# Seven block products for eight in half of a two-layer attention kernel

## The chip, the cores and the metric

The kernel runs on one core of a Trainium2 chip. The metric is the device time of one launch in microseconds (us). TensorE multiplies, VectorE and ScalarE do the elementwise work, GpSimd masks and issues loads, SyncE (SP) and ScalarE issue other transfers. Inputs and outputs are float32.

## The reference

Two attention layers over their own input, each with 2048 rows, 1024 columns, 32 heads of 32, side by side in the output:

```python
qkv = x @ wqkv                     # 2048x1024 @ 1024x3072
# layer A: each row attends to itself and 7 earlier rows, 2 apart
idx = pos[:, None] - arange(8)[None, :] * 2
logits = einsum("bhsd,bhswd->bhsw", q, k[idx]) * 32 ** -0.5     # idx < 0 masked
# layer B: each row attends to itself and the 255 rows before it
scores = einsum("bhqd,bhkd->bhqk", q, k) * 32 ** -0.5           # other keys masked
out = (softmax(...) applied to v) @ wo                          # @ 1024x1024
return concatenate([a, b], axis=-1)
```

## The kernel before, in words

**Units.** Rows are cut into units of 512. Units 0 to 3 are layer B (dense: a head needs 256 keys for a row), units 4 to 7 are layer A. Layer A's rows are put in another order on the host, even rows first, so that "2 apart" becomes "neighbours": units 4 and 5 are the even rows, 6 and 7 the odd ones. Features are worked on in eight groups of 128, which are four heads each; in this text one such group of one unit is a "head".

**Projections.** A float32 value is split in a high part (a cast to fp32r) and a low part (the difference), and each product is three matmuls: high-high, high-low, low-high (`TERMS`). For a unit, each of the 8 feature groups takes a product for q and one for k (L518, 8 pieces of 128 of the contraction times three terms, 512 columns: 24 matmuls), the values v come in three parts (L583, with 512 or 256 columns), and 8 output products (`o_items`, L645, 24 matmuls each) multiply the attention's results by `wo`. `qk_items`, `v_items` and `o_items` write these. A product fills one PSUM bank; there are three banks for products (`7 - NS`), four for scores, one for a head's values.

**The stream.** Weights and x come from DRAM through one stream (class `Stream`) with three buffers `raw` of 128x1024 (512 KB, `NRAW`). `load_to` issues a load on GpSimd's queue (L159), `split_to` casts what has landed (L201 on ScalarE or L204 on VectorE) and subtracts for the low part (L207 on VectorE). A buffer is loaded again once it has been split.

**Attention.** A head of layer A (`window`): scores (L711, 128 matmuls of 32x40), a mask added (L719), softmax on four passes over 128x640 on VectorE and an exponential on ScalarE (L735 to L747), a transpose (L749), eight copies on ScalarE that spread the weights (L758, L761), 40 matmuls with v (L774). Two sets of buffers alternate. The result is copied (L822, high part on ScalarE) and its low part made (L826, VectorE), and stays in SBUF for the output products. q, k and v of layer A stay on the chip too.

**The order.** The kernel is written out by a planner while it is built. It keeps a clock for each engine from fixed costs, holds four sequences (projections `gemm`, first and second halves of heads, others), and always puts next on TensorE what can start first by its clocks. What follows a product (eviction, low parts, sums) is written when the clocks say it is due. On the chip each engine then runs its instructions in that fixed order and waits on semaphores where data is late.

```python
def copy_out(dst, ps, bank, ring):
    if max(ck.free["act"], ck.now) + 0.48 <= max(ck.free["dve"], ck.now) + 0.6:
        nc.scalar.copy(dst, ps)
```

`copy_out` is an example: whether ScalarE or VectorE empties a bank is settled by the planner's clocks.

Of the kernel before, what the change touches and what calls it, by code (L numbers as in the profile page):

```python
# [25 lines left out]
LIGHT, LIGHT_FROM = 0.5, (4, 1)  # L26
# [8 lines left out]
TAIL, XAT = 4, 1  # L35
# [95 lines left out]
class Stream:  # L131
# [3 lines left out]
    def __init__(self, nc, ck, raws, wpool, xpool, items, more, light):  # L135

        self.nc, self.ck, self.raws, self.wpool, self.xpool, self.more = nc, ck, raws, wpool, xpool, more
        self.items = items
        self.raw, self.tiles, self.ready = {}, {}, {}
        self.loaded = self.split = 0  # L140
        self.light = light
        self.load_to(NRAW + len(more))

    def load_to(self, n):
        while not self.loaded:
# [7 lines left out]
            self.loaded = 2  # L153
        while self.loaded < min(n, len(self.items)):
            k = self.loaded - NRAW
# [3 lines left out]
            (self.nc.scalar if early else self.nc.gpsimd).dma_start(raw if len(ap.shape) == 2 else raw.rearrange("p (a b) -> p a b", a=2), ap)  # L159
            self.raw[self.loaded] = raw, (self.ck.load if early else self.ck.fetch)("load", self.ck.now)  # L160
            self.loaded += 1

    def split_to(self, n):
        while not self.split:
            (rx, tx), (rw, tw) = self.raw.pop(0), self.raw.pop(1)
            self.tiles[0], self.ready[0], self.ready[1] = [], [], []
            w = self.tiles[1] = self.wpool.tile([P, 2, 1024], F32R, tag="w", name="w")
            for h in range(2):
                c = slice(h * S, h * S + S)
                self.tiles[0].append(self.xpool.tile([P, 2, S], F32R, tag="x", name="x"))  # L170
# [5 lines left out]
        while self.split < min(n, len(self.items)):  # L176
            i = self.split
            self.load_to(i + 1)
            raw, t0 = self.raw.pop(i)
            if self.items[i][0] != "w":  # L180
                self.tiles[i], self.ready[i] = [], []
                for h in range(2):
                    t = self.xpool.tile([P, 2, S], F32R, tag="x", name="x")
                    self.ready[i].append(self.parts(t, raw[:, h * S:(h + 1) * S], t0, i < SIDE))
                    self.tiles[i].append(t)
            else:
                t = self.wpool.tile([P, 2, 1024], F32R, tag="w", name="w")
# [3 lines left out]
            end = self.ready[i] if self.items[i][0] == "w" else max(self.ready[i])  # L191
# [18 lines left out]

    def get(self, i):
# [5 lines left out]
def kernel(ctx, tc, xs, wqk, wv, wo, outs, units):  # L217
# [3 lines left out]
    U = len(units)  # L221
    units, xs = [units[i] for i in ORDER], [xs[i] for i in ORDER]
# [3 lines left out]
    wpool = ctx.enter_context(tc.tile_pool(name="wpool", bufs=3))  # L226
    xpool = ctx.enter_context(tc.tile_pool(name="xpool", bufs=NX))
    natp = ctx.enter_context(tc.tile_pool(name="natp", bufs=NN))
    pickp = ctx.enter_context(tc.tile_pool(name="pickp", bufs=1))
    opool = ctx.enter_context(tc.tile_pool(name="opool", bufs=NO))  # L230
# [13 lines left out]
    for u in range(U):  # L244
        for s in range(NG):
            if u and s in O_SLOTS:
                plan += [("o", u - 1, n) for n in O_SLOTS[s]]
# [4 lines left out]
        if u + 1 < U:  # L252
            plan.append(("x", u + 1))
    plan += [("o", U - 1, n) for n in range(NG)]
    items, where = [], {}

# [13 lines left out]
    for p in plan:  # L270
        ly = units[p[1]][0]
        if p[0] == "o":
            item(p, "w" if p[1] < U - 1 or p[2] < 3 else "xw", wo[ly, p[2]])
# [8 lines left out]
        elif p[0] == "qk":  # L282
            for t in range(2):
                if p + (t,) not in where:
                    item(p + (t,), "w", wqk[ly, 2 * p[2] + t])
        else:
            if NG - 1 in V_SLOTS:
                item(("qk", p[1], 0, 0), "w", wqk[units[p[1]][0], 0])
                unit_x(p[1])
            else:  # L290
                unit_x(p[1], 0)
                item(("qk", p[1], 0, 0), "w", wqk[units[p[1]][0], 0])
                unit_x(p[1], 1, 2, 3)
# [3 lines left out]
    st = Stream(nc, ck, raws, wpool, xpool, items, [more[:, 1024 * i:1024 * i + 1024] for i in range(3)],  # L297
                where[("qk",) + LIGHT_FROM + (0,)] if LIGHT_FROM[0] < U else len(items))

# [831 lines left out]
```

## Time and profile before

| | |
|---|---|
| median of 3 runs | 1833.96 us (1833.75 to 1835.53) |
| span of the profiled execution | 1830.6 us |
| that execution's own time | not given; the median is 3.4 above the span |
| TensorE busy | 1807.8 us, 99% |
| VectorE, ScalarE, GpSimd busy | 1202.9, 889.4, 394.4 us |
| DMA | 257.43 MB, mean 141 GB/s |
| layer A's part | from about 1030 us to the end |

The page first gives each engine's busy time and its share of the span; then the span in forty slices; then the DMA queues; then the chain of work that ended last, followed back from the end, by engine and line; then the groups of instructions, with busy time, mean and the idle time ahead of them. "L518" is line 518 of the kernel. Other views (busy time by window, the timeline, groups with shapes kept apart) are answers of the same trace.

### The profile page before, as it was taken

What the parts mean: (1) busy time and instruction counts of PE and PEld (TensorE: products, weight loads), DVE (VectorE), ACT (ScalarE), POOL (GpSimd) and SP (SyncE); (2) the same over time, 40 slices, a digit from 0 to 9 for tenths busy, and PEclk for the clock granted to TensorE, in tenths of its full rate; (3) what the DMA queues carried; (4) which work ended last, traced back from release to release, by engine and by line L of the source; (5) the groups of instructions that cost most, each with busy time, mean ns of one, the idle gap of its engine ahead of it and who ended that gap; (6) DMA issues with size and microseconds to landing.
All of it is one profiled execution on the core that took longest, in us unless ns stands there. A gap on an engine that the chain in (4) does not pass through costs nothing.

```text
span 1830.6 us, 38331 instructions
## 1 busy us (share of the span) xinstructions
PE 1807.8 (99%) x14826; PEld 1477.5 (81%) x14826; DVE 1202.9 (66%) x2694; ACT 889.4 (49%) x2254; POOL 394.4 (22%) x926
## 2 busy tenths in 40 slices
PE   9999999999999999999999999999999999999998
PEld 7787777888778888788887788888888788888887
DVE  6677886768867669777777564655547445655463
ACT  5556466565655655656555343433425234423331
POOL 3322323233242324332233200110001000100000
PEclk9999999999999999999999999999999999999999
DMA  8455665545656456455554343444334443534432
GB/s 242 121 138 139 176 164 150 170 121 160 164 155 164 136 151 183 125 157 141 141 142 130 110 135 116 152 143 130 119 115 143 133 138 108 162 107 128 127 104 83
DMA packets 109141, 257.43 MB, mean 141 GB/s; under 512 B 14496, under 2 KB 29856, under 8 KB 108960
## 3 DMA queue, kind: packets, MB, share of 16 engines
q0 software_dynamic: 41760, 152.06, 28.1%
q1 hardware_dynamic: 56832, 83.00, 17.6%
q10 hardware_dynamic: 10368, 19.93, 3.0%
q8 instruction: 117, 1.92, 0.5%
q14 instruction: 64, 0.52, 0.1%
HBM read 164.63 MB, written 23.07 MB: 103 GB/s over the span
## 4 chain that ended last, share of the span: by engine, by line
PE 92%; DVE 4%; DMA 2%; ACT 2%; issue 1%; SPq 0%; ACTq 0%; POOL 0%; DVEq 0%; POOLq 0%
PE g L518 37%; PE g L645 19%; PE g L583 17%; PE s L940 5%; PE s L857 5%; PE o L987 5%; PE s L711 2%; PE o L774 2%; DMA raw<-xs 1%; DVE w L207 1%; DVE s L862 1%; ACT s L867 0%; DMA qst<-nat 0%; DMA pbuf<-nat 0%; DVE x L207 0%
## 5 line engine op out<-in xcount | busy, mean ns | idle before, releaser
L518 PE MATMUL g<-x,w 128*128 128x512 f32 x3072 | 770.2, 394 | 3.8 <-DVE nm L729 2.4
L518 PEld LDWEIGHTS g<-x,w 128*128 128x128 f32 x3072 | 566.3, 189 | 114.2 <-issue 8.3
L583 PE MATMUL g<-w,x 128*128 128x256 f32 (+1 forms) x2304 | 391.9, 320 | 0.9 <-issue 0.7
L207 DVE TENSOR_TENSOR w<-raw,w 128x512 fp32r<-128x512 f32 x516 | 338.6, 698 | 52.0 <-ACT w L201 44.8
L583 PEld LDWEIGHTS g<-w,x 128*128 128x128 f32 x2304 | 332.3, 190 | 29.2 <-DVE w L207 1.8
L645 PE MATMUL g<-ot,w 128*128 128x512 f32 x1416 | 343.6, 393 | 3.7 <-DVE ot L826 1.8
L867 ACT ACTIVATE s<-s,nm 128x384 f32<-128x384 f32 (+2 forms) x512 | 274.3, 536 | 102.1 <-DVE nm L862 101.8
L862 DVE CUSTOM_DVE_ANT_0 s<-s,mask_d 128x384 f32<-128x384 f32 (+2 forms) x512 | 261.5, 553 | 88.2 <-PE s L857 87.5
L645 PEld LDWEIGHTS g<-ot,w 128*128 128x128 f32 x1416 | 262.4, 188 | 59.3 <-DVE ot L826 3.2
L926 POOL TENSOR_SCALAR_AFFINE_SELECT pbuf<-pbuf 128x128 f32<-128x128 f32 (+1 forms) x606 | 219.8, 391 | 325.1 <-ACT pbuf L947 323.8
L947 ACT ACTIVATE pbuf<-s 128x384 f32<-128x384 f32 (+2 forms) x480 | 202.7, 505 | 72.2 <-PE s L940 70.2
L159 POOL DMA_DIRECT2D raw<-wqk x126 | 68.1, 540 | 457.5 <-DVE w L207 356.3
L204 DVE CAST w<-raw 128x1024 fp32r<-128x1024 f32 x205 | 141.7, 691 | 24.8 <-PE g L518 24.0
L940 PEld LDWEIGHTS s<-qst,kst 128*128 128x128 f32 x704 | 113.0, 188 | 41.2 <-ACT s L867 16.3
L857 PE MATMUL s<-kst,qst 96*128 96x384 f32 (+2 forms) x512 | 142.4, 342 | 0.9 <-ACT s L867 0.6
L940 PE MATMUL s<-qst,kst 128*128 128x256 f32 (+2 forms) x704 | 136.5, 302 | 3.5 <-ACT s L867 3.0
L719 DVE TENSOR_TENSOR band<-s,near 128x160 f32<-128x160 f32 x128 | 32.4, 315 | 158.0 <-PE s L711 158.0
L536 ACT COPY ost<-g 128x512 f32<-128x512 f32 x54 | 31.7, 587 | 207.1 <-PE g L645 200.4
L857 PEld LDWEIGHTS s<-kst,qst 96*128 96x128 f32 x512 | 93.4, 189 | 26.2 <-issue 4.7
L826 DVE TENSOR_TENSOR ot<-o,ot 128x512 fp32r<-128x512 f32 x64 | 44.0, 688 | 101.6 <-ACT ot L822 101.4
L867 ACT ACTIVATION_READ_ACCUMULATOR s<-s,nm 128x1 f32 x512 | 105.3, 206 | 0.0
L159 POOL DMA_DIRECT2D raw<-wo x64 | 34.2, 534 | 304.2 <-DVE w L207 260.2
(77 smaller groups left out, 1298.6 us busy)
## 6 DMA issues: line engine op xcount, KB each, us to landing
raw<-wqk POOLq DMA_DIRECT2D x126, 512.0 KB, 4.3
raw<-wv POOLq DMA_DIRECT2D x72, 512.0 KB, 5.1
raw<-wo POOLq DMA_DIRECT2D x64, 512.0 KB, 4.1
qst<-nat SPq DMA_DIRECT2D x96, 256.0 KB, 5.3
kst<-nat SPq DMA_DIRECT2D x96, 256.0 KB, 5.6
raw<-xs POOLq DMA_DIRECT2D x28, 512.0 KB, 4.6
outs<-ost ACTq DMA_DIRECT2D x56, 256.0 KB, 2.3
kst<-halo SPq DMA_DIRECT2D x72, 128.0 KB, 4.5
```

The costliest lines, as they stand in the source:

```text
L159: (self.nc.scalar if early else self.nc.gpsimd).dma_start(raw if len(ap.shape) == 2 else raw.rearrange("p (a b) -> p a b", a=2), ap)
L204: nc.vector.tensor_copy(t[:, 0, :], raw)
L207: nc.vector.tensor_tensor(t[:, 1, c:c + 512], raw[:, c:c + 512], t[:, 0, c:c + 512].bitcast(F32), op=ALU.subtract)
L518: nc.tensor.matmul(h["ps"], h["w"][:, a, k * P:(k + 1) * P], xt[u][k][:, b, :], start=(k == 0 and i == 0), stop=(k == NK - 1 and i == 2))
L583: nc.tensor.matmul(ps, xt[u][kw * g + k][:, a, p0:p0 + P], h["w"][g][:, c, k], start=(first and t == 0 and half == 0), stop=(last and t == 2),
L645: nc.tensor.matmul(h["ps"], w[:, a, c:c + P], ot[u, k][:, b, :], start=(k == 0 and i == 0), stop=(k == NK - 1 and i == 2))
L857: nc.tensor.matmul(ps[:, :n], q[0:96, j, b * P:(b + 1) * P], kk[0:96, j, c0:c1], start=True, stop=True)
L862: nc.vector.tensor_tensor_reduce(ps[:, :n], ps[:, :n], mask[:, cut:full], scale=-1.0, scalar=BIG, op0=ALU.add, op1=ALU.min, accum_out=nm)
L867: nc.scalar.activation(ps[:, :n], ps[:, :n], AF.Exp, bias=nm, scale=-1.0, accum_out=sm)
L926: nc.gpsimd.affine_select(w, w, pattern=[[0, m], [step, n]], compare_op=ALU.is_ge, fill=0.0, base=base, channel_multiplier=chan)
L940: nc.tensor.matmul(ps[:, i * n:(i + 1) * n], kk[:, j, 256 + kb * P:256 + (kb + 1) * P], q[:, j, q0:q0 + n], start=True, stop=True)
L947: nc.scalar.activation(w, ps[:, :pack * n].rearrange("p (j n) -> p j n", j=pack), AF.Exp)
```

## The change

Layer A's products are made in Strassen's manner. The rows of two units (1024 rows: units 4 and 5 are the first pair, 6 and 7 the second) and the 1024 x 1024 matrices of q with k, of v and of `wo` are cut into 2 x 2 blocks. In place of eight block products there are seven (Winograd's form): four sums of blocks on each side, seven products, and seven sums of the results.

```python
PRODUCTS = (("11", "11"), ("12", "21"), (0, 3), (2, 2), ("22", 1), (3, 0), (1, "22"))
PAIRS = {"x": ((0, 1), (2, 3), (5, 6), (4,)), "o": ((0, 1), (4,), (2, 3), (5, 6))}
GROUPS = (("q", (0, 1, 2)), ("v", (0, 1, 2, 3)), ("q", (3, 4, 5)), ("q", (6, 7)))
FIRST = (("q", (0, 1, 2)), ("q", (3, 4, 5)), ("q", (6, 7)), ("d", (0, ..., 7)), ("v", (0, 1, 2, 3)))
PACE = ((70, 5.0), (154, 2.0))
SUMS = (("21", "+22", "-11"), ("12", "-S0"), ("11", "-21"), ("21", "+22"))
```

- **Groups.** A product of blocks is worked off in groups: 4 pieces of the contraction x 3 terms = 12 matmuls of 512 columns into one PSUM bank. "q" has 8 groups a product (q and k together), "v" and "o" (outputs) 4. `PAIRS` sets the order of products (numbers 0 to 6, "p0" to "p6"), two at a time; `GROUPS` the order within such a two. A pair's q, k and v are 84 groups, its outputs 28. The order is: q, k, v of the first pair (groups 0 to 91, the 8 output products "d" of layer B's last unit among them); of the second pair (92 to 175); outputs of the first (176 to 203), of the second pair (204 to 231). `FIRST` is the order at the first two products of the first pair: all q and k, then "d", then v.
- **Sums of weights** are made by VectorE during layer B (`spare_sums`, 24 tasks of two loads, four sums and a store) and for `wo` in two background lanes from the last dense head on, and kept in DRAM (`td`).
- **Sums of x and of attention results** (`SUMS`, four per pair and side) are made when they are needed: the blocks come through the stream's three `raw` buffers and `combine` adds or subtracts them in place (L256). Sum 0 is stored to DRAM too (`keep_sum`) and loaded again for sum 1 ("-S0").
- **Evictions.** `evac` copies a group out of its bank (L999) or adds it to an accumulator in SBUF (L1005); where two products are added to one another they stay in one bank.
- **Through DRAM.** q, k and v go to DRAM (`qkd`, `vd`) and are fetched for each head (`fetch`), not earlier than `PACE` allows: a head of the first pair every 5 groups from group 70, of the second pair every 2 groups from group 154. Attention results go to DRAM (`od`), are loaded again through the stream and split there (in layer B, L822 and L826's way stays).
- **Due times.** Each entry of the stream has a group number from which on it is split or summed; `phase_done` is called at the end of each group, behind `evac`; for the eight output products "d" it is called ahead of `copy_out`.

```diff
+    def combine(self, raw, t0, sign):
+        part, t1 = self.part
+        self.nc.vector.tensor_tensor(raw, part, raw, op=ALU.add if sign == "+" else ALU.subtract)
+        return raw, self.ck.use("dve", 1.25, t0, t1, port=True)
...
+            if self.items[i][0] == "p":
+                self.part = raw, t0
...
+            if self.items[i][0] in "+-":
+                raw, t0 = self.combine(raw, t0, self.items[i][0])
...
+            out += [(max(free, use[k][0] - S_AHEAD), use[k][0], 1, k + (z,)) for z in range(2)]
...
+    def keep_sum(raw, t, kind, u, z):
+        nc.sync.dma_start(sums[kind, u][:, 2 * z:2 * z + 2, :], raw.rearrange("p (a b) -> p a b", a=2))
...
+                if u == DU - 1:
+                    phase_done(phases.index(("d", u, n)))
                 o = stp.tile([P, S], F32, tag="ost", name="ost")
                 e = copy_out(o, h["ps"], h["b"], rg)
...
+            for t, (a, c) in enumerate(TERMS):
+                if b == "v":
+                    l, r = x[:, a, P * n:P * n + P], w[:, c, :]
+                else:
+                    l, r = w[:, a, P * k:P * k + P], x[:, c, :]
+                nc.tensor.matmul(h["ps"], l, r, start=(half == 0 and k == 0 and t == 0), stop=(k == 3 and t == 2),
+                                 skip_group_check=True)
+
+        def after(k):
+            if k < 3:
+                return
+            evac(kind, u, p, b, n, h)
+            phase_done(f)
...
+        if p == 0:
+            e = move(a)
+        elif p == 1:
+            o, key = out_tile()
+            e = move(o)
+            put(0, 0, o, e, key)
+        elif p == 2:
+            e = add(acc_u(b, n), a)
+        elif p == 3:
+            e = add(a, a)
...
+    def phase_done(f):
+        bg["at"] = f + 1
+        st.split_to(upto[f])
+        fetch()
...
+            if max(hg - 2, last_dense) not in done["scores"] or any((m,) + x not in done["c"] for x in need) or \
+                    bg["at"] < first + step * (r * NG + s):
+                break
...
-    n = TAIL
-    tail = [gemm[len(gemm) - NG * NK + i * NK:len(gemm) - NG * NK + (i + 1) * NK] for i in range(NG)]
...
+    for f, ph in enumerate(phases):
+        gemm += o_items(ph[1], ph[2]) if ph[0] == "d" else phase_items(f)
```

In `combine`, `part` is the block that came first. The work in layer B (units 0 to 3) keeps its order, with the weights' sums between.

More of the change, by code (lines that the diff above doesn't have):

```diff
@@ new lines, with landed @@
+    qkd = {(u, g): dram.tile([P, 2, 2 * S], F32, name=f"qk{u}_{g}") for u in range(DU, U, 2) for g in range(NG)}
+    vd = {(u, j): dram.tile([P, 8, S], F32, name=f"vd{u}_{j}") for u in range(DU, U, 2) for j in range(2)}
+    done = {}
+    for k in ("stack", "v", "o", "ot", "out", "nat", "second", "clear", "scores", "s", "t", "c"):
+        done[k] = {}
+    gates = {}
+    def landed(key, *which):
+        return lambda: all(done[key].get(w, ck.now + 1) <= ck.now for w in which)
+    phases = []
@@ L354 @@
     halo = [[dram.tile([P, 2, 256], F32, name=f"halo{i}_{s}") for s in range(NG)] for i in range(2)]
[L356 to L359 removed]
+    xt, xready, ot, rows, waiting = {}, {}, {}, {}, {}
     class Ring:
```

588 lines of the change are left out of this document (479 added, 109 removed).

## The prediction

> **What bounds the kernel now.** I read the page first, then the busy time by stretch, then the groups by form, then single stretches of the timeline.
>
> ```profile
> span 1830.6 us, 38331 instructions
> PE 1807.8 (99%) x14826; PEld 1477.5 (81%) x14826; DVE 1202.9 (66%) x2694; ACT 889.4 (49%) x2254; POOL 394.4 (22%) x926
> ...
> PE 92%; DVE 4%; DMA 2%; ACT 2%; issue 1%; SPq 0%; ACTq 0%; POOL 0%; DVEq 0%; POOLq 0%
> ```
>
> TensorE is busy for 1807.8 of 1830.6 us and holds 92% of the chain that ended last. Only 22.8 us are idle, so nothing but fewer or cheaper matmuls can shorten this kernel, and every new pause of TensorE is paid in full. The busy time of layer A alone, from 1030 us to the end (each row: the window, then busy time and instructions of PE, PEld, DVE, ACT and POOL, the granted clock, the share of the DMA engines, GB/s):
>
> ```profile
> 1442.00:1640.00 198.00, 195.61 (x2141) 162.37 (x2140) 109.50 (x188) 73.21 (x138) 20.55 (x37) 1.00 0.43 130
> ...
> sum 801.00, PE 789.44 PEld 656.57 DVE 440.45 ACT 293.20 POOL 77.20; mean PE 197.36 PEld 164.14 DVE 110.11 ACT 73.30 POOL 19.30
> ```
>
> There TensorE has 789 of 801 us, VectorE 440 (55%), the DMA engines a share of 0.43 in the row shown. The other engines have room; the question is whether the new work can use it without holding up TensorE.
>
> **What is removed.** The groups of TensorE between 1442 and 1640 us, and one row of the chain:
>
> ```profile
> L518 PE MATMUL g<-x,w 128*128 128x512 f32 x373 | 87.8, 392 | 0.0
> ...
> L583 PE MATMUL g<-w,x 128*128 128x256 f32 x192 | 23.9, 284 | 0.0
> ...
> 1688.17 10.88 PE g L518 x48
> ```
>
> Forty-eight matmuls of 512 columns take 10.88 us in a row, 0.2267 each; one of 256 columns costs 23.9/192 = 0.1245. In the listing of the built program the 512-column products of x, weights and attention outputs number 5376 before and after, and the 256-column ones fall from 1536 to 768: layer A had 2688 of the wide and 768 of the narrow, and has 2688 wide, exactly seven eighths. So the change does what it says, and TensorE loses 768 x 0.1245 = 95.6 us. The attention's own matmuls are unchanged in number. If nothing else happened, the span would be 1735.0.
>
> **What is added, and why it lies on the path.** A group now has 12 matmuls, 2.7 us. There are three PSUM banks for groups, so TensorE can run about two groups, 5.4 us, past an eviction that doesn't come. Evictions, and the sums of x or of attention outputs (`combine`, 1024 columns on VectorE), stand in one order on VectorE and ScalarE. `phase_done` issues all sums that are due by then in one go, each behind its load, and there are only three buffers for loads. This is ScalarE's and VectorE's order at the first such place, with the loads on GpSimd, from the listing (not a profile):
>
> ```
> ACT  902 L243 TensorCopy x<-raw 128x512 [waits DMASW4_49,DVE_49]
> ACT  904 L243 TensorCopy x<-raw 128x512 [waits DMASW7_49,DVE_49]
> ACT  906 L718 TensorCopy ost<-g 128x512 [waits DMAHW2_49]
> DVE  1927 L256 TensorTensor raw<-raw 128x1024 [waits DMASW4_49,DVE_49]
> DVE  1930 L256 TensorTensor raw<-raw 128x1024 [waits DMAHW5_49,DMASW7_49,DVE_49]
> POOL 737 L182 DMACopy raw<-xs 128x1024 [waits DMASW3_49,DVE_49]
> POOL 738 L182 DMACopy raw<-xs 128x1024 [waits DMAHW5_49,DMASW4_49,DVE_49]
> ```
>
> The eviction at 906 had its data long before, but stands behind four casts, the last two of which wait for a sum (1930), that waits for a load (738), that waits for the store of the previous sum out of the same buffer (DMAHW5). That a ready instruction sits behind a waiting one is seen in the trace of before too:
>
> ```profile
> 1716.78 0.59 ACT L822 CAST ot<-o 128x512 fp32r<-128x512 f32 x1 [5.08 <-PE o L774]
> ...
> 1718.34 1.29 DVE L207 TENSOR_TENSOR w<-raw,w 128x512 fp32r<-128x512 f32 x2 [3.29 <-ACT w L201]
> 1719.55 0.68 DVE L826 TENSOR_TENSOR ot<-o,ot 128x512 fp32r<-128x512 f32 x1
> ```
>
> L826's input was there at 1717.37; it ran at 1719.55, behind L207 that waited 3.29 us for another cast. The prices of the steps:
>
> ```profile
> DMA to landing us min/median/max: 3.6/4.5/9.3
> ...
> outs<-ost ACTq DMA_DIRECT2D x56, 256.0 KB, 2.3
> ...
> L747 DVE TENSOR_TENSOR band<-band,sm 128x640 f32<-128x640 f32 x32 | 26.4, 825 | 1.1
> ...
> L826 DVE TENSOR_TENSOR ot<-o,ot 128x512 fp32r<-128x512 f32 x64 | 44.0, 688 | 101.6 <-ACT ot L822 101.4
> ...
> L201 ACT CAST x<-raw 128x512 fp32r<-128x512 f32 x31 | 17.8, 618 | 22.7 <-DMA raw<-xs 19.9 <-DVE x L204 2.6
> ```
>
> A load of the stream (512 KB) lands 4.5 us after its issue; ends 3.6 and, under load, 6. A sum of 1024 columns: 0.825 x 1024/640 = 1.3 (no such operation was in the trace; between 0.7, one cast of that width, and 1.4, two of L826; the row of the same kind decides). Two casts 1.2, their low parts run beside or behind. A store of 512 KB is bounded by one of 256 KB (2.3) and a load (4.5); I take the middle, 3.4. An eviction with an add is L826's 0.69, a copy 0.6.
>
> The first place, from the end of the last output group of layer B: two weight splits on VectorE until a buffer is free 2.6, load 4.5, sum 1.3, store 3.4, load 4.5, sum 1.3, casts 1.2, eviction 0.6: 19.4, of which TensorE covers 5.4. It stands for 14.0.
>
> The other places of this stage (three, where two sums of two parts come due together) have one load inside: eviction 0.7, sum 1.3, load 4.5, sum 1.3, casts and one low part 1.9, eviction 0.7 make 10.4, less 5.4: 5 each, 15. First pair's q, k and v: **29**.
>
> In the second pair's q, k and v the same four places have an attention head's matmuls beside them (2.5, below), and at the first of them the first sum's loads are early: 0.7 + 2.6 + 3.4 + 4.5 + 1.3 + 1.2 + 0.6 - 7.9 = 6.4, the others 10.4 - 7.9 = 2.5 each: **14**.
>
> The first pair's outputs: four sums of two and three parts come due within three groups. Load, sum, store, load, sum, low parts, half a softmax that stands between (1.65), eviction: 4.5 + 1.3 + 3.4 + 4.5 + 1.3 + 1.9 + 1.7 + 0.7 - 7.9 = 11.4; a second load and sum behind it, 5.8; two later places 2.5 to 5 each, 7: **24**.
>
> The end of layer B: the last banded head now has only 21 matmuls of the output product beside it, since `FIRST` puts all q and k groups before and the v groups behind. Its second half, two rounds of scores, ScalarE and values, takes some 16 us, TensorE's own part of that is 8: **8** idle.
>
> **The end of the kernel.** The last output products need every head of the second pair. In the listing the last five heads' values stand with only three product matmuls between them. A head's chain:
>
> ```profile
> L719 DVE TENSOR_TENSOR band<-s,near 128x160 f32<-128x160 f32 x128 | 32.4, 315 | 158.0 <-PE s L711 158.0
> ...
> L749 DVE STREAM_TRANSPOSE band<-band 128x1024 f32<-128x1024 f32 x32 | 39.9, 1245 | 1.1
> ...
> L758 ACT COPY wide<-band 32x512 f32<-32x512 f32 x128 | 79.1, 618 | 32.0 <-DVE band L749 30.6
> ...
> L761 ACT COPY wide<-band 32x128 f32<-32x128 f32 x128 | 37.9, 296 | 1.7
> ...
> 1737.13 1.32 PE L711 MATMUL s<-pbuf 32*32 32x40 f32 x128
> ...
> 1752.97 1.18 PE L774 MATMUL o<-wide,vbuf 128*32 128x8 f32 x40
> ```
>
> Scores 1.32, four masks 1.26, four passes of 640 columns on VectorE 3.3, transpose 1.25, eight spreads 3.66, values 1.18: 12.0. Exponential, reciprocal and a dozen handovers aren't in it; I take 2 for them, an estimate: 14. That lies between 12.0 and the 17.0 that this head took beside projections (1737.13 to 1754.15). Two buffers make two heads alternate, so from the values of the fifth-last head to those of the last are two rounds, 28, with 9.4 of TensorE's work: 18.6. Then copy 0.6, store 2.3, three issues on GpSimd, loads 4.5, casts, low part: 10. Then one product runs (10.9), while behind its first group stand both sums for the next pair: load, load, sum, sum, store, load, sum, store, load, sum, load, sum, low parts, eviction. From the start of that product: 4.9 + 4.5 + 2.6 + 3.4 + 4.5 + 1.3 + 3.4 + 4.5 + 1.3 + 4.5 + 1.3 + 1.4 + 0.7 = 38.3, less 10.9: 27.4. Two more places of 5: 10. Together **66**.
>
> VectorE's and ScalarE's total: VectorE gains 168 evictions with an add (116), 40 sums (52), 16 further adds (11), 70 low parts (48), 96 small sums in layer B, and loses about 100 us of casts, low parts and copies; in layer A 440 becomes about 570 of 705. I price that at nothing on average; if it fills up, see the rivals. The small sums in layer B and their 48 loads I take at nothing too, between 0 and 5, as VectorE idles there for a quarter of the time (1202.9 - 440 busy in 1030).
>
> **The clock.** After a long pause TensorE restarts slowly:
>
> ```profile
> 10.00:15.00 5.00, 4.78 (x13) 3.56 (x14) 4.58 (x8) 3.66 (x6) 1.90 (x3) 0.66 0.98 345
> ...
> 1705.00:1715.00 10.00, 7.62 (x192) 6.19 (x191) 3.21 (x7) 1.28 (x3) 0.00 (x0) 1.00 0.24 85
> ```
>
> At 10 to 15 us the granted clock was 0.66 after a broken start, a loss of 1.7 us; the longest later pause, 2.4 us in 1705 to 1715, cost nothing. Nine pauses of the list are longer than 4 us: 9 x 1.7 = **15**. The Trainium skill ("TensorE: Matmul & The Clock Gate", What's actually happening) halves the clock after at least one idle window of about 3.4 us that runs free; by it about half of the pauses near 5 us would escape, and the term would be 10.
>
> **Sum.** 1830.6 - 95.6 + 8 + 29 + 14 + 24 + 66 + 15 = 1891. The median of the runs shown, 1833.96, lies 3.4 above the span; the forecast is **1894**. A page speaks for less: by the Trainium skill ("DMA: Bandwidth & Descriptors", Anatomy of one DMA) a transfer takes 2.0 us and its bytes at 436 GB/s, 3.2 for 512 KB. The loads of the trace say 4.5 with a minimum of 3.6; with 3.2 on some 23 loads in line the sum would be 30 less, 1864, still slower.
>
> **Rivals.**
> First, on the other side: the sums are hidden. If loads land before VectorE comes to the sums, as nearly all loads of before do (POOL waits for buffers there, not TensorE for data), a place takes less than the 5.4 us that the banks cover, and only the end of layer B, the last heads with their restart and half of the last chain remain: 1830.6 - 95.6 + 8 + 28.6 + 14 + 7 + 3.4 = 1796. Against it: with three buffers the second half's loads can't be issued before the first half's sums are done, and the store lies between. It decides if a place is shorter than 5.4. Chance 0.16.
>
> Second: VectorE becomes the bound from the second pair's heads on. There, 140 us of its work stands against 116 of TensorE's in the last four stretches of eight groups, on top of its waits for loads; a tenth more on some 350 us of attention stages is 35: 1929. For it: 80% on average against 55% before, and a head that waits holds TensorE's order. Chance 0.20.
>
> Third: loads under load. 367 MB are moved instead of 255, layer A at about 240 GB/s; but 345 GB/s were moved at 10 to 15 us at a share of 0.98. At 5.5 us a load, 23 more: 1917, inside the range and no case of its own.
>
> **How the numbers follow.** The forecast has 0.64. Its own range: loads at 3.6 and no clock loss give -21 - 15, places covered by a head -15: 1843; loads at 6 and a store like a load +45: 1940. To leave out no more than 2 in 10 (the first rival, and what lies above the second) the range is 1820 to 1950. Over 0.2%, which is about what a measurement of this kernel can tell: faster 0.15, slower 0.83, between 0.02.
>
> **What would show it.** The 256-column rows of L583's successor should number 768, and TensorE's busy time be near 1712 with the span far above. The waits should show TensorE's L983 held by evictions (L999, L1005, L718) for 100 us or more, and VectorE's L256 by loads. Windows of the first eight v groups of layer A and of the last 100 us should show TensorE at half. I am wrong if L983's idle time is below 90 us in all, if L256 never waits for a DMA, or if single loads land in less than 3.5 us.

## The result and the profile after

The changed kernel took 2003.47 us (median, 1998.73 to 2006.64), the one before 1834.74 beside it: 1.0916 times as long, interval 1.0903 to 1.0929. Slower was forecast, but 1894, in a range that ended at 1950. Spans of the same kernel's profiled executions lay at 2004.9, 1989.4 and 1997.2 us in three runs, so what is read from one profile is good to some 10 us in the total; the comparisons below go by ratios.

The page of after: the span, each engine's busy time, and TensorE's busy share and granted clock in forty slices:

```profile
span 2004.9 us, 38063 instructions
...
PE 1781.6 (89%) x14058; PEld 1425.3 (71%) x14058; DVE 1353.1 (67%) x2901; ACT 948.2 (47%) x2296; POOL 507.5 (25%) x1136
...
PE   9999999999999999999989588999897999578338
...
PEclk9999999999999999999998789999999999789578
```

TensorE is idle for 223.3 us (22.8 before) and busy for 26 less. The matmuls saved would have made that 96 less; but the clock is below full in many slices, and a matmul at half the clock takes twice as long (5 in 2 us instead of 10, last section): busy time times the missing share of the clock, summed over windows of 2 us, is 62 us, 1.6 before. So of 174.3 us more span, 200.5 are pauses, 60 slow matmuls, 9 unexplained, less 95.6.

The waits of TensorE in layer A (who waited for what: us in total, times, the longest):

```profile
PE g L983 <- DVE acc L1005: 83.2, 12, 29.6
PE o L1243 <- ACT wide L1232: 24.0, 11, 8.5
PE g L983 <- ACT w L265: 16.3, 2, 10.5
PE g L983 <- ACT ost L718: 15.6, 1, 15.6
PE g L983 <- DVE ost L1001: 15.6, 1, 15.6
PE s L1181 <- issue: 9.4, 4, 3.7
PE g L983 <- ACT wide L999: 7.7, 1, 7.7
PE g L983 <- ACT acc L999: 5.2, 1, 5.2
```

L718, L999, L1001 and L1005 are evictions: 127 us are waits for a bank to be emptied, few and long. VectorE's and ScalarE's own waits in the same part say what stood in their queues. VectorE's sums (L256) waited for loads, and its low parts of weights (L272), the largest row, for ScalarE's casts (L265); ScalarE's casts of x and of attention results (L243) waited for the sums:

```profile
DVE w L272 <- ACT w L265: 74.9, 58, 15.4
DVE raw L256 <- DMA raw<-od: 41.2, 14, 5.2
DVE raw L256 <- DMA raw<-xs: 27.3, 8, 5.9
```

```profile
ACT x L243 <- DVE raw L256: 187.1, 28, 14.4
```

These rows don't say which of these waits held up which eviction; the timeline does, place by place.

The first such place in the timeline (start, duration, engine, instruction; in brackets the idle time before it and what ended it):

```profile
1104.69 5.60 PE L825 MATMUL g<-r,w 128*128 128x512 f32 x24
1116.09 0.79 PE L983 MATMUL g<-w,x 128*128 128x512 f32 x1 [5.81 <-ACT w L265]
1118.06 7.04 PE L983 MATMUL g<-w,x 128*128 128x512 f32 x23 [1.18 <-DVE w L272]
1140.70 9.65 PE L983 MATMUL g<-w,x 128*128 128x512 f32 x32 [15.60 <-ACT ost L718]
```

The engines that feed it, in the same stretch: GpSimd's load issues, VectorE, ScalarE.

```profile
1114.92 0.55 POOL L182 DMA_DIRECT2D raw<-xs  x1 [0.27 <-DVE w L272]
1119.17 0.55 POOL L182 DMA_DIRECT2D raw<-xs  x1 [3.69 <-DVE w L272]
1121.13 0.53 POOL L182 DMA_DIRECT2D raw<-xs  x1 [1.42 <-DVE w L272]
1127.85 0.53 POOL L182 DMA_DIRECT2D raw<-xs  x1 [6.19 <-DVE raw L256]
1129.11 0.53 POOL L182 DMA_DIRECT2D raw<-xs  x1 [0.73 <-DVE raw L256]
1133.99 0.53 POOL L182 DMA_DIRECT2D raw<-xs  x1 [4.35 <-DMA sx<-raw]
```

```profile
1126.33 2.49 DVE L256 TENSOR_TENSOR raw<-raw 128x1024 f32<-128x1024 f32 x2 [5.74 <-DMA raw<-xs]
1129.50 1.29 DVE L249 TENSOR_TENSOR x<-raw,x 128x512 fp32r<-128x512 f32 x2 [0.68 <-ACT x L243]
1135.03 1.23 DVE L256 TENSOR_TENSOR raw<-raw 128x1024 f32<-128x1024 f32 x1 [4.24 <-DMA raw<-xs]
1137.77 1.23 DVE L256 TENSOR_TENSOR raw<-raw 128x1024 f32<-128x1024 f32 x1 [1.52 <-DMA raw<-xs]
```

```profile
1128.85 1.14 ACT L243 CAST x<-raw 128x512 fp32r<-128x512 f32 x2 [9.59 <-DVE raw L256]
1139.03 1.14 ACT L243 CAST x<-raw 128x512 fp32r<-128x512 f32 x2 [9.05 <-DVE raw L256]
1140.08 0.58 ACT L718 COPY ost<-g 128x512 f32<-128x512 f32 x1
```

The bank that L718 empties at 1140.08 had been full since 1110.3, when layer B's last output product ended (1104.69 + 5.60). ScalarE reached it after two pairs of casts, each behind a sum, the second behind the store of a sum (`sx`) and a load.

### The profile page after: what moved, and what is told of

Read it like the earlier page. It is cut to its first block, busy times and chain, and to the rows that moved or that the text cites. A ratio compares the mean times of both kernels' runs of the same rounds, so it can differ in the third digit from the quotient of the medians.

```text
span 2004.9 us, 38063 instructions
## 1 busy us (share of the span) xinstructions
PE 1781.6 (89%) x14058; PEld 1425.3 (71%) x14058; DVE 1353.1 (67%) x2901; ACT 948.2 (47%) x2296; POOL 507.5 (25%) x1136
## 2 busy tenths in 40 slices
DMA packets 187160, 369.57 MB, mean 184 GB/s; under 512 B 21344, under 2 KB 79712, under 8 KB 186976
## 5 line engine op out<-in xcount | busy, mean ns | idle before, releaser
L983 PE MATMUL g<-x,w 128*128 128x512 f32 x2016 | 509.0, 411 | 117.0 <-DVE acc L1005 76.9
L983 PEld LDWEIGHTS g<-x,w 128*128 128x128 f32 x2016 | 397.1, 199 | 210.3 <-ACT w L265 55.1
L696 PE MATMUL g<-x,w 128*128 128x512 f32 x1536 | 407.1, 397 | 3.4 <-ACT x L243 2.2
L696 PEld LDWEIGHTS g<-x,w 128*128 128x128 f32 x1536 | 281.3, 189 | 51.3 <-ACT x L243 2.6
L265 ACT CAST w<-raw 128x1024 fp32r<-128x1024 f32 x101 | 105.9, 1049 | 210.7 <-PE g L983 114.3
L765 PE MATMUL g<-w,x 128*128 128x256 f32 (+1 forms) x1152 | 203.5, 323 | 0.7 <-DVE w L249 0.6
L272 DVE TENSOR_TENSOR w<-raw,w 128x512 fp32r<-128x512 f32 x224 | 144.5, 687 | 83.7 <-ACT w L265 83.1
L983 PE MATMUL g<-w,x 128*128 128x512 f32 x672 | 167.7, 408 | 34.2 <-ACT ost L718 15.6
L825 PE MATMUL g<-r,w 128*128 128x512 f32 x768 | 191.0, 396 | 1.4 <-ACT r L1316 1.1
L765 PEld LDWEIGHTS g<-w,x 128*128 128x128 f32 x1152 | 169.7, 192 | 13.9 <-DVE w L249 1.5
L983 PEld LDWEIGHTS g<-w,x 128*128 128x128 f32 x672 | 131.2, 197 | 65.8 <-ACT ost L718 16.0
L243 ACT CAST x<-raw 128x512 fp32r<-128x512 f32 x114 | 64.6, 617 | 220.0 <-DVE raw L256 187.1
L825 PEld LDWEIGHTS g<-r,w 128*128 128x128 f32 x768 | 143.8, 190 | 30.3 <-ACT r L1316 1.8
L1444 PEld LDWEIGHTS s<-qst,kst 128*128 128x128 f32 x704 | 113.7, 190 | 48.2 <-ACT s L1371 14.2
L1005 DVE TENSOR_TENSOR acc<-g,acc 128x512 f32<-128x512 f32 x136 | 91.0, 684 | 68.8 <-PE g L983 68.7
```

The source lines that it names most:

```text
L272: nc.vector.tensor_tensor(lo[:, b], raw[:, b], hi[:, b].bitcast(F32), op=ALU.subtract)
L696: nc.tensor.matmul(h["ps"], h["w"][:, a, k * P:(k + 1) * P], xt[u][k][:, b, :], start=(k == 0 and i == 0), stop=(k == NK - 1 and i == 2))
L765: nc.tensor.matmul(ps, xt[u][kw * g + k][:, a, p0:p0 + P], h["w"][g][:, c, k], start=(first and t == 0 and half == 0), stop=(last and t == 2),
L825: nc.tensor.matmul(h["ps"], w[:, a, c:c + P], ot[u, k][:, b, :], start=(k == 0 and i == 0), stop=(k == NK - 1 and i == 2))
L983: nc.tensor.matmul(h["ps"], l, r, start=(half == 0 and k == 0 and t == 0), stop=(k == 3 and t == 2), skip_group_check=True)
L1444: nc.tensor.matmul(ps[:, i * n:(i + 1) * n], kk[:, j, 256 + kb * P:256 + (kb + 1) * P], q[:, j, q0:q0 + n], start=True, stop=True)
```

## The experiments

Ratios are to the kernel before in the same set of runs. The changed kernel itself had 1.0916, then 1.0902 (1.0875 to 1.0929) and 1.0912 (1.0886 to 1.0938); 0.01 is 18 us. Theory A is the prediction's: loads and sums in line hold up evictions. Its main rivals: VectorE's total is the bound, or the transfers are.

**The sums left out**, and with them the store of the first one.

```diff
-        parts = [a] if isinstance(a, str) else SUMS[a]
+        parts = [a] if isinstance(a, str) else SUMS[a][:1] if kind == "x" else SUMS[a]
```

> The sums of x are left out: each of the four takes its first block alone, so products 2, 3, 5 and 6 of q, k and v are of single blocks and the output is not the reference's. Everything else stays: the sums of weights, the sums of attention results, the order of products, stores and heads. Theory A (loads, sums and the store of sum 0 stand in line ahead of evictions, and the clock is halved behind each pause): of the changed kernel's pauses of TensorE, 32.5 us at four places of the first pair's q, k and v and 19.3 us in the second pair's go, but for some 5 to 10, and with them 15 to 20 us of the slow clock: 2003 falls by 50 to 70, to about 1945. Rival B (VectorE, or the split of weights through the same three buffers, sets the pace there): the pauses stay with other names and it falls by under 15, to about 1990.

Measured: 1953.47 us, 1.0664 (1.0633 to 1.0695): 45 us less, just short of the 50 expected and far from the rival. The same edit for `"o"`:

> The sums of attention results are left out in the same way: products 2, 3, 5 and 6 of the outputs are of single blocks, and the output is not the reference's. Theory A: in the first pair's outputs most of 38.9 us of pauses, in the second pair's 29.6 and 9.9 us go, and some 15 us of the slow clock; 10 to 20 us of load latency stay: 2003 falls by 65 to 85, to about 1928. Rival B (the second pair's heads bound both stages, so that TensorE only waits elsewhere): the first pair's 38.9 turn into waits for heads, only the last 39 go, and it falls by about 40, to about 1963.

Measured: 1917.46 us, 1.0468 (1.0412 to 1.0523): 81 us less, as theory A has it. Added up (they were not left out together) the two are three quarters of the 169 us lost. Leaving sums out takes loads, stores and VectorE's work away alike, so it names the place and not the mechanism.

**The order.** All sums stay; they go into the queues when their loads have landed by the planner's clock, or else when the first product needs them.

```diff
     def phase_done(f):
...
-        st.split_to(upto[f])
+        st.split_landed(upto[f])
...
+    def split_landed(self, n):
+        while self.split < min(n, len(self.items)):
+            self.load_to(self.split + 1)
+            if self.split not in self.raw or self.raw[self.split][1] > self.ck.now:
+                return
+            self.split_to(self.split + 1)
```

> Nothing is taken out. At the end of a group the casts and sums that are due are put into the queues only when by the planner's clock their load has landed, and otherwise when the first product needs them; before, all that was due went in at once, ahead of the next eviction. Theory A1 (evictions stand behind sums that wait for loads): the 15.6 us at the first sums go, and some 10 to 20 more at other places: 2003 falls by 20 to 40, to about 1975. Rival A2 (three buffers and the chain load, sum, store, load bind, in whatever order): the wait moves to the product that needs the sum, and it stays within 10 of 2003.

Measured: 1946.78 us, 1.0634 (1.0619 to 1.065): 51 us less, more than A1 expected. At the first place TensorE now runs through:

```profile
1116.05 23.62 PE L990 MATMUL g<-w,x 128*128 128x512 f32 x95 [1.18 <-DVE w L279]
```

and no wait for an eviction is left among the long ones (L250 and L272 are the casts of x and of weights, L279 the low parts of weights, L990 the products):

```profile
PE g L990 <- ACT x L250: 48.9, 12, 10.5
PE g L990 <- ACT w L272: 41.7, 7, 9.2
PE g L990 <- DVE w L279: 13.2, 14, 2.0
```

The same 14058 matmuls and the same 369.57 MB cost 51 us less when the casts and sums stand elsewhere in the queues. The planner replanned around them (VectorE has 26 instructions more, ScalarE 12 fewer), so it isn't quite the order alone. Rival A2 is right in part: TensorE's idle time fell from 223.3 to 163.1 us, so of 127 us of waits for evictions about half went, and the other half moved to products that wait for their own operands, 104 us in the three rows shown.

**Sums of x ahead, more buffers, plain outputs.** Three edits, one on the other, all on top of the run before:

```diff
+    X_OPS = ((3, 2, 3, ALU.add), (2, 0, 2, ALU.subtract), (0, 3, 0, ALU.subtract), (1, 1, 0, ALU.subtract))
...
+        if kind == "x" and not isinstance(a, str):
+            items.append(("x", xd[u][:, a, 2 * z:2 * z + 2, :]))
...
+            q = self.loaded - self.late
+            raw = self.more[k] if 0 <= k < len(self.more) else self.extra(q % 8 - 3) if q >= 0 and q % 8 > 2 else self.raws.tile([P, 1024], F32, tag="raw", name="raw")
...
+PLAIN = ((0, 1), (7, 8), (9, 10), (11, 12))
+        for i, pair in enumerate(PLAIN if kind == "o" and u == DU + 2 else PAIRS[kind]):
```

> The kernel of the run late, and besides the four sums of x of each pair are made during layer B, by the same tasks as the sums of weights (16 more tasks: two loads, four sums, a store), and kept in DRAM; layer A loads them ready. The output is the reference's. Theory A (sums of x in line with evictions are what the first and second pair's q, k and v wait for): against late, 20 to 35 us of pauses and 8 us of slow clock go, 5 come back in layer B: ratio to the kernel before from 1.063 to about 1.047, 1917 us. Rival (loads of weights through three buffers bind, or layer B pays for the 16 tasks what layer A gains): 1.058 to 1.065.

> The run lx, and besides the stream has eight buffers instead of three from the first pair's outputs on: five more in the memory of q, k and v's accumulators, which are done by then. Theory A (in the outputs a sum of three blocks fills all three buffers, so that load, sum, store and load follow one another): 25 to 40 us of the pauses in both output stages go: ratio about 1.030, 1888 us. Rival (the second pair's heads or VectorE's total bind there): not more than 8 us.

> The run lxo, and besides the second pair's outputs are eight block products again instead of seven (32 groups of 12 matmuls instead of 28, no sums, no accumulators; unit 6's first, which need only its own heads). Theory A: 4 x 2.7 = 11 us more matmuls, but the products of unit 6 cover unit 7's heads (24 us of pauses) and the chain of sums behind the last head goes (10 to 20 left of it): 20 to 35 us less than lxo, ratio about 1.015, 1860 us. Rival (VectorE sets the pace of the heads whatever TensorE does meanwhile): the heads end as late, and it is at most 10 us less or up to 10 more.

The unedited kernel ran in the same set:

> The changed kernel once more, unedited, on the same chip as the three below, so that they can be compared within one set: 1.0916 times the kernel before, some 2000 us.

Measured: 1998.23 us, 1.0902, and of the three:

| run | us | ratio | step |
|---|---|---|---|
| lx, x's sums made in layer B | 1900.05 | 1.0362 (1.0335 to 1.0389) | -50 us from late |
| lxo, eight buffers in the outputs | 1858.33 | 1.0146 (1.0125 to 1.0167) | -40 us |
| lxop, second pair's outputs plain | 1843.64 | 1.0071 (1.0048 to 1.0094) | -14 us |

The first step came out higher than expected, the second at the upper end, the third below its range: TensorE's 11 us of extra matmuls are paid, and in the two profiles the last head's values came only 6 us earlier (1760.5 against 1766.5). The second step speaks most plainly against VectorE or the transfers as the bound: it moves the same 373.78 MB, takes 9 of 1365 us of work from VectorE, and gives 40 us.

**Layer B.** The weights' sums left out, those of `wo` in the background lanes too:

```diff
-            return td[b][:, t, n, :]
+            t = ("11", "12", "21", "22")[t]
...
-             "tasks": [("q", g, z) for g in range(NG) for z in range(2)] + [("v", k, z) for k in range(4) for z in range(2)]}
+             "tasks": []}
...
-                for n in range(4):
+                for n in range(0):
```

> The changed kernel without the sums of weights: the 24 tasks in layer B and the four of the background lanes are left out, and layer A loads single blocks of the weights in their place, so the output is not the reference's. Theory A (the tasks' four operations on VectorE and their transfers stand between layer B's steps): of 14 us more pauses and 5 us of slow clock before 1010 us most goes: 12 to 18 us less than the changed kernel, ratio about 1.081. Rival (the prediction's: between 0 and 5, since VectorE has room): ratio 1.087 to 1.091.

Measured: 1981.28 us, 1.0827 (1.0799 to 1.0856): 16 us less, in theory A's range. It isn't all found in layer B. The busy time of TensorE in the first 1010 us (one row for before, then the sums of the same window for after and without the weights' sums),

```profile
0.00:1010.00 1010.00, 998.34 (x6009) 805.39 (x6010) 753.93 (x1936) 588.20 (x1688) 307.87 (x763) 1.00 0.56 153
```

```profile
sum 1010.00, PE 984.39 PEld 791.38 DVE 763.36 ACT 578.93 POOL 317.50; mean PE 984.39 PEld 791.38 DVE 763.36 ACT 578.93 POOL 317.50
```

```profile
sum 1010.00, PE 991.42 PEld 801.35 DVE 738.03 ACT 587.32 POOL 303.37; mean PE 991.42 PEld 801.35 DVE 738.03 ACT 587.32 POOL 303.37
```

shows that of 14 us more pauses (998.34 less 984.39) half come back. The slow clock in this window doesn't go: 1.6 us before, 6.4 in after, 6.8 without the sums. What the rest of the 16 is stays open. On GpSimd instead of VectorE (on top of lxop; `nc.gpsimd.tensor_tensor` in the tasks' sums) the tasks cost more:

> The run lxop with the tasks' sums of weights and x in layer B (160 operations of 128x256) on GpSimd instead of VectorE. Theory A (they delay the steps of softmax that stand behind them on VectorE): some 10 of 17 us that layer B lost come back: ratio about 1.001. Rival (GpSimd's masks and load issues are then delayed instead, or the transfers are what disturbs): no gain or slower, 1.007 to 1.03.

Measured: 1858.87 us, 1.0161 (1.0145 to 1.0176), 16 us slower than lxop. One operation of 128x256 takes 0.74 us there against 0.43 on VectorE (medians), and GpSimd issues the stream's loads too; which of the two hurts wasn't tried apart.

**The clock.** Fillers that keep TensorE at work in nine pauses:

```diff
+FILL = {24: 22, 26: 64, 33: 30, 45: 15, 57: 12, 212: 40, 216: 125, 219: 20, 225: 14}
...
+            if k == 0 and f in FILL:
+                ps, bank = rs.take()
+                wide_id = cst["ident"][:, None, :].to_broadcast([P, 4, P])
+                for i in range(FILL[f]):
+                    nc.tensor.matmul(ps, cst["ident"], wide_id, start=True, stop=True)
+                rs.give(bank, ck.now)
```

> Nothing is taken out. At the nine longest pauses where no head needs the score banks (the first pair's start and the last products) 14 to 125 extra matmuls of 128x512 on constants go into a free score bank ahead of the group that waits, each series about 1 us shorter than the pause that was measured there, so that they hold up nothing. All other instructions keep their order. Theory A (after a pause TensorE runs at half its clock for some microseconds): in the changed kernel's rows, busy time times the share of the clock that is missing is 20 us at these places; it falls by 15 to 20, to about 1985, and the granted clock at 1105 to 1265 us is 1.0. Rival B (the loss behind pauses isn't the clock's, or the clock isn't set by the pause): no change, 2003, or slower by what the fillers take.

Measured: 1998.18 us, 1.0917 (1.0899 to 1.0935), no change that can be told. Beside the unedited kernel, in more rounds:

> The changed kernel unedited, beside the next one, in five rounds: 1.090 times the kernel before.

> The run warm again, in five rounds beside the unedited one on the same chip. In its profile the loss by the clock fell by 8 us in the first pair's q, k and v and by 3 to 7 in the last products, yet its time was not below the changed kernel's. If a slow stretch behind a pause is paid in full (theory A), 10 to 15 us less than the run beside it, ratio about 1.084; if the sums' chain sets the pace, so that a slow TensorE mostly shortens its next wait (theory B), 0 to 6 us less.

Measured: 1996.42 us, 1.0904 (1.0886 to 1.0922) against 1998.94, 1.0912 (1.0886 to 1.0938): 1.5 us less, within theory B and within the noise. The first pair's stage in the two profiles, without and with fillers (the column behind POOL is the granted clock):

```profile
1090.00:1310.00 220.00, 181.31 (x871) 146.43 (x869) 108.55 (x161) 47.93 (x63) 45.73 (x84) 0.91 0.60 193
```

```profile
1090.00:1310.00 220.00, 211.68 (x1186) 172.22 (x1185) 111.63 (x168) 52.97 (x72) 46.95 (x87) 0.99 0.62 199
```

The clock is back at 0.99, and the loss by the clock, summed as above, falls from 9.9 to 1.7 us in this stage and from 14.3 to 7.3 behind 1850 us. The rows alone don't say who is ahead: of the 315 matmuls more, 143 are fillers and the rest is work that came into the window earlier. Both profiles begin the first v group within 0.1 us of one another (1117.28 and 1117.36), and the instructions' order is fixed, so the same instruction can be compared. The scores of layer A's second head, without and with fillers:

```profile
1312.73 1.42 PE L1181 MATMUL s<-pbuf 32*32 32x40 f32 x128
```

```profile
1305.87 1.42 PE L1188 MATMUL s<-pbuf 32*32 32x40 f32 x128
```

So with fillers TensorE is 6.9 us ahead here, and 9.8 at the next head: in this stage the slow matmuls had been paid about in full. The lead is still 9.4 us at 1470, then shrinks, to 0.9 at 1691 and to nothing at 1763. Behind the last head 6.7 us are won again, so that these two profiles end 6.1 us apart, though the medians don't. (`warm` beside the first profile of after shows the same: 7.7 and 10.6 ahead, 2.5 at 1693.) What takes the lead back between 1470 and 1690 isn't shown. So at these places the slow matmuls were paid where they stood, but the fillers took away only 13 of 59 us of loss in all, and the time of a launch didn't follow clear of noise. What the other 46 cost wasn't tried.

**Towards a faster version**, on top of lxop: all outputs plain (`kind == "o"` without the condition on `u`), then the planner's estimates:

```diff
-SEAT_LATE = 4.0
+SEAT_LATE = 8.0
...
-                h["p"] = ck.use("act", 0.31, e)
+                h["p"] = ck.use("act", 0.31, e) + 2.0
```

> The run lxop with the first pair's outputs as eight block products too: seven for eight is left only in q, k and v. Theory A (the sums of attention results and the evictions with an add keep VectorE from the second pair's heads): 11 us more matmuls, but of 24 us of pauses and 8 us of slow clock between 1400 and 1660 us some 20 go: ratio to the kernel before from 1.007 to about 1.002. Rival (eight buffers already hide these sums, the pauses are the heads' own): 11 us slower, ratio 1.013.

> The run lxop with two of the planner's estimates changed: a head's rows count as landed 8 us after their last issue's estimate instead of 4, and its weights as ready 2 us later. Theory A (TensorE's fixed order puts scores and values ahead of products that could run, because transfers and VectorE are later than planned): 10 to 20 us of the 25 us of waits at scores and values go: ratio about 0.999. Rival (the heads' own chain is the bound, and products run out): same within 4 us, or slower.

> The two edits of the runs plain4 and later together (products of seven for eight in q, k and v alone; the heads' rows and weights planned later). If what is left is the planner's early placing of heads (theory A), the two gains add: 15 us and 21 us below lxop, ratio to the kernel before about 0.988, 1808 us. If both remove the same waits (rival B): about 0.995.

And the buffer of the first weights behind layer B's last outputs (`later4w`), then the estimates moved on to 12.0 and 4.0 (`later4x`):

```diff
-        i = c % 3 if c < n3 else (3, n3 % 3, (n3 + 1) % 3, (n3 + 2) % 3)[(c - n3) % 4]
+        i = c % 3 if c < n3 else (n3 % 3, (n3 + 1) % 3, (n3 + 2) % 3, 3)[(c - n3) % 4]
...
-            j = i - 3 if i < n else n - 1 if i == n else i - 4
+            j = i - 3 if i < n + 3 else n - 1 if i == n + 3 else i - 4
```

> The run later4, and besides the first weights of v behind layer B's last output products go into a buffer that is free three products earlier, instead of the attention results' memory. Theory A: the two pauses of 5.8 and 1.2 us at 1107 us and 2.4 us of slow clock behind them go: 8 to 9 us below later4, ratio about 0.983. Rival: the load itself is late, not the buffer, and 3 us are gained at most.

> The run later4w with the estimates moved on: rows 12 us instead of 8, weights 4 us instead of 2. Theory A (placing is too early still): another 3 to 6 us. Rival (by 8 and 2 heads are placed rightly, and later ones leave TensorE without products at the end): same or slower by up to 10.

| run | us | ratio |
|---|---|---|
| plain4, Strassen in q, k, v alone | 1828.02 | 0.9989 (0.9973 to 1.0005) |
| later, heads planned later | 1822.63 | 0.9957 (0.9941 to 0.9974) |
| later4, both | 1816.95 | 0.9917 (0.9894 to 0.994) |
| later4w, and the weight buffer | 1809.13 | 0.987 (0.9848 to 0.9892) |
| later4x, estimates moved on | 1824.16 | 0.9953 (0.9938 to 0.9969) |

plain4 gave 15 us although it adds 11 us of matmuls; later 21, the top of what was expected. Together they gave 28, between "add" (36) and "the same waits" (21). The buffer gave the 9 expected. Moving the estimates on cost 15 us, more than the rival's 10: the best of the three settings tried is 8 and 2. later4w lies 1.3% below the kernel before. The planner's estimates weren't tried on the kernel before, which has the same two; without them (plain4) the difference from it is not clear of noise. An estimate of what they could give there at most is its whole idle time, 22.8 us, nearly the 24 that later4w is ahead; so how much of the 1.3% is due to seven for eight isn't shown. The page of later4w:

```profile
span 1811.3 us, 38187 instructions
...
PE 1760.8 (97%) x14154; PEld 1415.8 (78%) x14154; DVE 1321.4 (73%) x2918; ACT 951.2 (53%) x2300; POOL 493.9 (27%) x1107
```

and the group that had waited for 151 us in after (117.0 and 34.2 in its two forms):

```profile
L983 PE MATMUL g<-x,w 128*128 128x512 f32 x2016 | 509.0, 411 | 117.0 <-DVE acc L1005 76.9
...
L983 PE MATMUL g<-w,x 128*128 128x512 f32 x672 | 167.7, 408 | 34.2 <-ACT ost L718 15.6
```

```profile
L1022 PE MATMUL g<-x,w 128*128 128x512 f32 x2112 | 505.3, 395 | 4.4 <-ACT wide L1038 1.5 <-issue 1.2 <-ACT x L257 0.7
...
L1022 PE MATMUL g<-w,x 128*128 128x512 f32 x672 | 158.6, 394 | 1.9 <-DVE wide L1044 1.9
```

waits for 6.3 us, and the mean of a matmul is back from 411 to 395 ns.

## Why the prediction was right or wrong

The direction and the mechanism (evictions behind sums that wait for loads) were right, the size was not: 156 us of additions were forecast, 269.9 came (2004.9 less 1735.0). Of the signs named, three came: L983 idle for 151 us, L256 waiting for loads, loads of 4.6 and 5.0 us. TensorE's busy time near 1712 did not (1781.6).

**What is removed: right.** The 256-column matmuls are 768, all in layer B now. Busy time is 1781.6 and not 1712 because of the slow clock (60 us) and 9 us that I can't place.

**Places: right, but for three that the list lacks.** Predicted and measured length, from the timeline of after:

| place | predicted | measured pauses |
|---|---|---|
| first pair's q, k, v | 14 + 15 | 15.6, 7.7, 4.4, 3.6, 1.2 = 32.5 |
| second pair's q, k, v | 14 | 5.2, 1.9, 3.2, 7.2, 1.8 = 19.3 |
| first pair's outputs | 24 | 15.6, 7.1, 7.5, 7.3, 1.4 = 38.9 |
| end of layer B | 8 | 3.6, 2.3 = 5.9 |
| last heads | 18.6 | 21.8 |
| restart, chain, two more | 10, 27.4, 10 | 10.5, 29.6, 5.8 + 4.2 |
| first weights of v | none | 5.8, 1.2 = 7.0 |
| heads' scores ("issue") | none | 9.4 |
| layer B before 1010 us | 0 | 14 |

**The terms that failed: the clock, and the length of the chains.** The additions were 114 us short. The clock has 45 of them: "Nine pauses of the list are longer than 4 us: 9 x 1.7 = 15", and the profile has 60. Both factors were low. The 1.7 came from a single broken start; layer A has 15 pauses of more than 4 us and loses 55 us by the clock behind 1010 us, 3.7 for each. Shorter pauses slow it too (below), and the short bursts of the last heads stay slow throughout (last section). The fillers show that in the first pair's stage and in the last products such a loss was paid where it stood; what of it the whole launch pays stays open.

The pauses at the places of the list came to 168 us, not 141, and the three places that it lacks to 30. Small pauses and busy time that I can't place are the rest. In the first chain the order of steps was right and its length was not: from the end of layer B's last product to the eviction I had 19.4 us, it was 30.4 (1110.3 to 1140.7). "Two weight splits on VectorE until a buffer is free 2.6, load 4.5" took 16.0: the three loads of the sum of three blocks came one at a time, at 1114.9, 1119.2 and 1121.1, as weights left the three buffers. That sum is two operations, 2.5 and not 1.3; the store took 5.2, between 1128.8 and 1134.0, against 3.4; the reload took 3.8 against 4.5, and the other steps about what their rows said. That the pause of 15.6 looks like the 14 forecast is luck: TensorE had waited 7.0 us before, in the same chain. In the last chain, 43.2 us against 38.3, the product that covered it took 13.6, begun at half clock, instead of 10.9. lxo's 40 us show what three buffers cost in the outputs.

**Layer B at nothing: wrong.** "Between 0 and 5, as VectorE idles there for a quarter of the time" stands against 14 us more pauses there; leaving out the weights' sums, with their transfers and those of `wo`, gave 16, of which 7 are found in layer B. An idle share of an engine was no ground for a term of nothing. Whether VectorE's work or the transfers cost it wasn't tried apart.

**Loads: nearly right.** 4.6 us for x, 5.0 for attention results, against 4.5. The Trainium skill's 3.2 us ("DMA: Bandwidth & Descriptors", Anatomy of one DMA) doesn't hold for these loads in this kernel, and 1864 by it was further off.

**The clock rule.** By the Trainium skill ("TensorE: Matmul & The Clock Gate", What's actually happening) the clock is halved after at least one idle window of about 3.4 us. The trace agrees only in part: the pause of 3.2 us before 1522 left the clock at 1.00 and that of 3.6 before 1248 was followed by 0.83, but a pause of 2.1 us before 700.4 was followed by 0.50, so 3.4 us is no safe limit here.

```profile
1520.00:1540.00 20.00, 17.28 (x231) 13.85 (x232) 15.31 (x26) 8.65 (x14) 2.66 (x5) 1.00 0.58 160
1240.00:1260.00 20.00, 16.38 (x60) 13.00 (x59) 10.30 (x16) 4.62 (x6) 6.59 (x11) 0.83 0.66 203
702.00:704.00 2.00, 2.00 (x11) 2.00 (x11) 1.94 (x4) 0.60 (x1) 0.00 (x0) 0.50 1.06 224
```

**Rivals.** The first (sums hidden) fell: L256 waits 68.5 us for loads. The second (VectorE) is not the bound: where VectorE is fullest in the second pair's heads, 41.2 of 50 us from 1610 on, TensorE is busy for 48.2, and where TensorE is idle for half of the time, in the 50 us from 1710 on, VectorE has 28.3; eight buffers, which take next to no work from it, gave 40 us. The third, transfers slower under load, is half a microsecond for the loads of these chains (5.0 against 4.5), and 1.8 for the one store that was followed.

## What to carry to other kernels

Work that waits for a transfer must not enter an in-order queue ahead of evictions that are ready: putting it in only when its data should have landed gave 51 us here, with the same matmuls and transfers. Count the buffers that a sum needs at once, and who holds them when it starts; three blocks and three buffers mean one load latency after another. And take an algorithm that saves matmuls only where its extra passes find cover: as tried here it cost time in the outputs (14 and 15 us less without it, lxop and plain4), and in q, k and v alone, with sums of x made ahead, it is even with the kernel before (plain4, 0.9989) or, with a better order, ahead of it (later4w, 0.987). And size the slow stretch behind pauses from more than one of them: 1.7 us each was forecast, 3.7 came.

## What the runs showed of the hardware

Matmuls behind a pause ran at a granted clock of 0.50 for a few microseconds: at 1118 us, after two pauses of 5.8 and 1.2 us, 5 matmuls in 2 us instead of 10.

```profile
1118.00:1120.00 2.00, 1.94 (x5) 1.55 (x6) 1.32 (x4) 1.05 (x1) 0.55 (x1) 0.50 0.83 313
...
1122.00:1124.00 2.00, 2.00 (x10) 1.66 (x9) 0.00 (x0) 0.00 (x0) 0.00 (x0) 1.00 0.93 270
```

And TensorE, busy for a third of the time in short bursts, didn't get its clock back during the last heads: the granted clock was 0.50 from 1860 to 1880.

```profile
1860.00:1880.00 20.00, 6.55 (x213) 4.83 (x213) 11.41 (x22) 10.85 (x22) 0.53 (x1) 0.50 0.29 92
```
